# Four loads of softmax denominators stand at other places in a DMA queue

## The chip, the core and the metric

The kernel runs on one core of one Trainium2 chip. The metric is the device time of one execution in microseconds (us), as a median of several runs. The core has five engines with instruction queues of their own: PE (matrix multiply), DVE (vector), ACT (activation functions and copies), POOL (general) and SP, which in this kernel does nothing but issue DMA transfers. Each engine takes its instructions in the order in which they stand in its queue. An instruction that waits for a semaphore holds up all that stand behind it on the same engine.

## The reference

One transformer block over 2048 tokens of width 512, with sliding-window attention (32 heads of 16, window 256) and a gated feed-forward layer, both with shift, scale and gate vectors `sa, ca, ga, sb, cb, gb` computed from a condition vector:

```python
qkv = (x @ wqkv).reshape(B, S, 3, H, Dh).transpose(2, 0, 3, 1, 4)
q, k, v = qkv[0], qkv[1], qkv[2]
scores = jnp.einsum("bhqd,bhkd->bhqk", q, k) * (Dh ** -0.5)
mask = (idx[:, None] - idx[None, :] >= 0) & (idx[:, None] - idx[None, :] < W)
p = _softmax(jnp.where(mask[None, None], scores, -1e9), axis=-1)
o = jnp.einsum("bhqk,bhkd->bhqd", p, v)
...
h = _layernorm(x, axis=-1) * (1 + ca) + sa
x = x + ga * _A_ref(h, A_wqkv, A_wo)
h = _layernorm(x, axis=-1) * (1 + cb) + sb
x = x + gb * _B_ref(h, B_w1, B_w3, B_w2)
```

## The kernel before

The attention is cut into 32 units. Unit u belongs to head group g = u // 4 (four heads) and token block b = u % 4 (512 tokens). A unit has three parts, which run in different unit times:

- `unit_a(u)` makes queries and keys: 12 products on PE (L489), three copies on ACT (L495 the raw product, L501 and L498 the rounded parts `qk1` and `qk0`), two subtractions on POOL (L507), and then six transfers on SP (L512) that lay the parts out in `ring`, the buffer that the score products read.
- `unit_b(u)` finds the row maxima: 16 score products on PE (L542), a reduction for each on DVE (L549), two small DVE steps (L557, L559), a transpose (L565), a copy on ACT (L570) and two small transfers into `ring` (L574).
- `unit_c(u)` computes scores again (L819) with the maxima subtracted, masks them on POOL (L847, L864) or DVE, takes the exponential on ACT (L840), multiplies with the values on PE (L780), copies the result on ACT (L887) and stores it on SP (L890) to the DRAM tensor `o_dr[b]`.

Each head's stored result has 17 useful rows: 16 of the output, and row 16 (`DH`) with the sum of the exponentials, the denominator of the softmax.

The three parts are interleaved by a table of numbers. Each step has a key, 8 for each unit time plus an offset, and the steps with keys under `TS` = 232 are written out in the order of their keys; that order is what each engine's queue holds. While unit u runs its part c, unit u + 2 runs part b and unit u + 3 part a. Steps with later keys, and all of the output projection and the feed-forward layer behind them, are put in order by a scheduler at build time, `Sched`. Between the attention steps stand small side jobs: a load (L947 or L961), some work on POOL (L948 or L957) and a store (L949 or L962) of a piece of a later weight.

`early_sums` issues four loads (L791), one for each token block b: from `o_dr[b]` the denominators of the 28 heads of the first seven groups, 112 rows of 128 numbers, into a quarter of the tile `wqr`. The last of these 28 heads is stored by unit 24 + b, with the key 8(24 + b) + 10.63. The load before stands at the key 8(24 + b) + 12.5, so it is the next SP instruction behind that store. The next steps on SP are the side job's load and the six transfers L512 of the next `unit_a`, whose keys lie 4.8 to 5.2 behind the store's.

The four quarters of `wqr` are read in the stretch that `Sched` orders: a reciprocal on DVE (L1163) for each b, a store of the result (L1164) to `r_dr[b]`, and from there loads (L1176) that spread it over the rows of the output, which is then multiplied with it ahead of the output projection (L1205).

The store's key, and the keys of L512 and of the load:

```python
at(t0 + X["o"][1], store, "store", (["os"], [("o_dr", b, g)], 0.5, 256))
...
for r in range(3):
    at(t0 + y["row"][r], lambda r=r: rows(r), "qk_rows")
```

with `X["o"][1]` = 10.63 and t0 = 8u in `unit_c`, and `X["row"]` = (8.681, 8.806, 9.018) and t0 = 8(u − 3) − 1.228 in `unit_a`.

Of the kernel before, what the change touches and what calls it, by code (L numbers as in the profile page):

```python
# [21 lines left out]
NB = 4  # L22
# [26 lines left out]
NU = NQ * NB  # L49
# [231 lines left out]
def us(t):  # L281
# [5 lines left out]
             job_dma=("SP", 0.5), scores=("PE", 0.2), top=("DVE", 0.5), parts=("DVE", 0.4), turn=("PE", 0.11), cut=("ACT", 0.16),  # L287
# [36 lines left out]
def block_kernel(ctx: ExitStack, tc: tile.TileContext, x, wqk, wv, wo, w13, w2, c, wmod, out):  # L324
# [400 lines left out]
    def at(t, fn, kind=None, use=None):  # L725
        ops.append((t, len(ops), fn, kind))
# [57 lines left out]
    def early_sums(at):  # L784

        lt = {}
        for b in range(NB):
            def load(b=b):
                if not lt:
                    lt[0] = a1.tile([P, D], F32, name="wqr", bufs=1)  # L790
                nc.sync.dma_start(lt[0][:16 * NQ - 16, b * P:b * P + P], o_dr[b].rearrange(  # L791
                    "(h r) t -> h r t", r=32)[:H - 4, DH].rearrange("h (s t) -> h s t", t=P))
            at(8 * (NU - 2 * NB + b) + 12.5, load, "job_dma")
        return lt

    def unit_c(u, t0, at):
# [194 lines left out]
    for u in range(NU):  # L991
# [10 lines left out]
        if u in (2, 14):  # L1002
            at(8 * u + 0.3, lambda u=u: copy_raw(u // 14))
    firsts = early_sums(at)
    ops.sort(key=lambda o: o[:2])
    last = [o for o in ops if o[0] >= TS]
# [687 lines left out]
```

## Time and profile before

| | us |
|---|---|
| median of 3 runs | 974.34 (974.3 to 975.61) |
| the profiled execution, its own time | 971.44 |
| its span in the profile | 969.4 |
| mean granted clock of PE in it | 0.993 of full |

The profile lists one execution. Times in its rows are microseconds from the start of the span. "SPq" rows are DMA issues on SP: the start and the time that issuing took, not the transfer itself. In square brackets stands how long an engine was idle before a row, and what released it. The granted clock is the share of full speed that PE's throttle gave. Attention runs from about 40 to 482 us; the first store L890 is at 113 us, the 28th (unit 27) at 438.6 us.

### The profile page before, as it was taken

How to read it: one execution, taken by the hardware profiler on the slowest of the kernel's cores; microseconds unless marked ns; L12 is line 12 of the kernel's file. 1: busy time of each engine (PE TensorE's matmuls, PEld its weight loads, DVE VectorE, ACT ScalarE, POOL GpSimd, SP SyncE). 2: the span in 40 equal slices, each digit the busy share in tenths (PEclk: the TensorE clock that was granted, in tenths of full speed). 3: DMA queues.
4: the chain of work that ended last, by engine and by line, in shares of the span. 5: the costliest groups of instructions: out<-in, count | busy, mean ns of one | idle time of the engine just before them, and what ended most of it. 6: DMA issues, size and time to landing. Idle time of an engine off the chain costs nothing.

```text
span 969.4 us, 17140 instructions
## 1 busy us (share of the span) xinstructions
PE 939.2 (97%) x5316; PEld 717.3 (74%) x5316; DVE 720.6 (74%) x2041; ACT 552.2 (57%) x1258; POOL 524.4 (54%) x734
## 2 busy tenths in 40 slices
PE   6999999999999999998899999999999999999998
PEld 2678777777777776664588778888888888888886
DVE  6575889899989898977667695667679765566545
ACT  3333888787878787765669854433446343433330
POOL 7321787777868686754643774368556332222320
PEclk9999999999999999998999999999999999999999
DMA  9521354444544444435893664575554523212002
GB/s 312 175 78 56 111 184 145 144 143 144 170 150 143 144 144 144 135 126 166 227 261 115 202 206 158 185 253 200 171 168 173 171 90 93 65 63 83 34 23 87
DMA packets 81559, 141.64 MB, mean 146 GB/s; under 512 B 10554, under 2 KB 23226, under 8 KB 81468
## 3 DMA queue, kind: packets, MB, share of 16 engines
q1 hardware_dynamic: 80748, 139.50, 44.4%
q10 hardware_dynamic: 720, 1.05, 0.3%
q8 instruction: 42, 0.69, 0.3%
q14 instruction: 49, 0.40, 0.2%
HBM read 85.72 MB, written 34.61 MB: 124 GB/s over the span
## 4 chain that ended last, share of the span: by engine, by line
PE 83%; POOL 6%; DVE 4%; DMA 3%; issue 2%; ACT 1%; SPq 0%; POOLq 0%; ACTq 0%; DVEq 0%
PE st L1469 11%; PE mx L1469 11%; PE mx L542 7%; PE pj L489 7%; PE st L819 7%; PE mx L1563 6%; PE po L780 6%; PE st L1563 6%; PE po L1469 4%; PE st L709 3%; PE pj L1469 3%; POOL pt L847 2%; PE po L1563 2%; POOL qk L507 2%; PE mx L1205 2%
## 5 line engine op out<-in xcount | busy, mean ns | idle before, releaser
L549 DVE CUSTOM_DVE_ANT_0 junk<-mx,mskq 128x384 bf16<-128x384 f32 (+2 forms) x503 | 251.9, 527 | 31.2 <-PE mx L542 29.6
L542 PE MATMUL mx<-ring 96*128 96x384 f32 (+1 forms) x503 | 152.7, 342 | 6.2 <-DMA ring<-qk 3.5
L819 PE MATMUL st<-ring 100*128 100x384 f32 (+2 forms) x488 | 148.8, 346 | 0.5 <-ACT pt L840 0.4
L847 POOL TENSOR_SCALAR_AFFINE_SELECT pt<-pt 128x256 f32<-128x256 f32 x268 | 108.6, 408 | 69.2 <-ACT pt L840 58.7
L489 PE MATMUL pj<-hT,wq 128*128 128x512 f32 x384 | 136.7, 406 | 1.2 <-DVE wq L478 0.8
L542 PEld LDWEIGHTS mx<-ring 96*128 96x128 f32 x503 | 92.8, 191 | 38.4 <-DVE mt L549 23.2
L840 ACT ACTIVATE pt<-st 128x256 f32<-128x256 f32 x263 | 94.7, 387 | 36.5 <-DVE st L837 28.8
L1513 POOL TENSOR_TENSOR t<-t,t 128x512 f32<-128x512 f32 x28 | 41.0, 1463 | 137.6 <-DVE t L1501 133.8
L819 PEld LDWEIGHTS st<-ring 100*128 100x128 f32 x488 | 91.8, 192 | 18.5 <-issue 6.7
L780 PE MATMUL po<-pt,vS 128*17 128x256 f32 (+2 forms) x1408 | 98.2, 391 | 2.3 <-POOL pt L847 1.8
L507 POOL TENSOR_TENSOR qk<-qkr,qk 128x512 fp32r<-128x512 f32 x64 | 83.2, 1300 | 27.6 <-ACT qkr L495 27.3
L837 DVE COPY_PREDICATED st<-later,st 128x128 f32<-128x128 uint8 x263 | 71.0, 291 | 13.1 <-PE st L819 10.3
L489 PEld LDWEIGHTS pj<-hT,wq 128*128 128x128 f32 x384 | 71.8, 191 | 10.2 <-issue 1.7
L1060 POOL TENSOR_TENSOR w<-w,w 128x512 fp32r<-128x512 f32 (+2 forms) x35 | 55.5, 1599 | 34.0 <-PE pj L1563 17.8
L780 PEld LDWEIGHTS po<-pt,vS 128*17 128x17 f32 x1408 | 32.8, 97 | 47.7 <-issue 21.7
L1501 DVE TENSOR_TENSOR t<-mx,t 128x512 f32<-128x512 f32 x54 | 36.9, 687 | 37.3 <-PE mx L1469 34.3
L1469 PE MATMUL st<-b,w 128*128 128x512 f32 x240 | 60.2, 390 | 1.4 <-ACT t L1508 1.4
L864 POOL TENSOR_SCALAR_AFFINE_SELECT sm<-sm 128x256 f32<-128x256 f32 x109 | 41.9, 406 | 30.1 <-ACT sm L854 26.1
L1469 PE MATMUL mx<-b,w 128*128 128x512 f32 x228 | 57.1, 391 | 0.0
L831 ACT ACTIVATE pt<-st 128x384 f32<-128x384 f32 (+2 forms) x109 | 45.6, 434 | 14.2 <-DVE st L827 12.7
L1469 PEld LDWEIGHTS st<-b,w 128*128 128x128 f32 x240 | 45.0, 188 | 11.4 <-ACT t L1508 1.8
L1501 DVE TENSOR_TENSOR t<-st,t 128x512 f32<-128x512 f32 x35 | 24.1, 689 | 37.0 <-PE st L1469 33.3
(322 smaller groups left out, 2093.4 us busy)
## 6 DMA issues: line engine op xcount, KB each, us to landing
ring<-qk SPq DMA_DIRECT2D x192, 128.0 KB
o_dr<-os SPq DMA_DIRECT2D x32, 256.0 KB
w<-wsum SPq DMA_DIRECT2D x14, 512.0 KB
w<-w2g SPq DMA_DIRECT2D x14, 512.0 KB
jb<-in_w SPq DMA_DIRECT2D x24, 256.0 KB
wraw<-in_w SPq DMA_DIRECT2D x7, 768.0 KB
w<-wraw SPq DMA_DIRECT2D x14, 384.0 KB
vS<-in_wmod SPq DMA_DIRECT2D x20, 256.0 KB
```

Source lines behind the costliest of these rows:

```text
L489: nc.tensor.matmul(v["ps"], WQ[g][w][:, n // 3], hTp(i, n // 3, b * BT, BT), start=(n == 0), stop=(n == 3 * KC - 1))
L507: nc.gpsimd.tensor_tensor(out=v[n], in0=v["raw"], in1=v[1].bitcast(F32), op=ALU.subtract)
L542: nc.tensor.matmul(v[i][:, :n], queries(NS, a, gq, 1), keys(NS, hh, a, k0, gq + 1 - k0), start=True, stop=True)
L549: nc.vector.tensor_tensor_reduce(out=junk[:, :n], in0=v[i][:, :n], in1=mskq[:, 3 * P - n:], scale=1.0, scalar=-3e38, op0=ALU.add, op1=ALU. ...
L780: nc.tensor.matmul(po[32 * i:32 * i + DH + 1, qb * P:(qb + nq) * P], vS[:, kb, 4 * g + i], pts[i // 2][:, i % 2, c0:c0 + nq], start=first, ...
L819: nc.tensor.matmul(ps[:, :nq], keys(NM, hh, a, kb, 1), queries(NM, a, kb, nq), start=True, stop=not plus)
L837: nc.vector.copy_predicated(ps[:, 0], later, ps[:, 2])
L840: nc.scalar.activation(pt_of(j, a)[:, hh, :2], v[j, a, hh][:, :2], AF.Exp, scale=SCALE)
L847: nc.gpsimd.affine_select(out=pt[:, :, 2 * m], in_=pt[:, :, 0], **w)
L1469: nc.tensor.matmul(ps(bk), WT[s, n][w][:, col], BB[t, k][r], start=start and c == 0, stop=stop and c == 5, skip_group_check=True)
L1501: return nc.vector.tensor_add(o, x, y)
L1563: nc.tensor.matmul(ps(bk), tiles[hk + (h,)][:, i * P:(i + 1) * P], w2_of(last, y, f), start=(m == 0), stop=(m == 5))
```

## The change

The four loads get later keys. For b = 0, 1, 2 the key is 8 larger, one unit time; for b = 3 it is 3.4 larger, 231.9, which is just behind the last of the transfers L512 (231.79) and just under `TS`.

```diff
@@ early_sums
                 nc.sync.dma_start(lt[0][:16 * NQ - 16, b * P:b * P + P], o_dr[b].rearrange(
                     "(h r) t -> h r t", r=32)[:H - 4, DH].rearrange("h (s t) -> h s t", t=P))
-            at(8 * (NU - 2 * NB + b) + 12.5, load, "job_dma")
+            at(8 * (NU - 2 * NB + b) + (20.5 if b < NB - 1 else 15.9), load, "job_dma")
         return lt
```

SP's queue in units 24 and 25, before. `o_dr_74` to `o_dr_77` are `o_dr[0]` to `o_dr[3]`; `x2` is two equal issues in a row:

```order
L890 DMA o_dr_74<-os 128x512
L791 DMA wqr<-o_dr_74 112x1x128
L961 DMA jb_6935<-in_w 128x512
L512 DMA ring<-qk_6865 16x4x512 x2
L512 DMA ring<-qk_6831 16x4x512 x2
L512 DMA ring<-qk_6873 16x4x512 x2
L949 DMA w2g<-jb_6702 128x512
L574 DMA ring<-mT_7015 4x4x128 x2
L890 DMA o_dr_75<-os 128x512
L791 DMA wqr<-o_dr_75 112x1x128
L961 DMA jb_7170<-in_w 128x512
L512 DMA ring<-qk_7100 16x4x512 x2
```

And the same place now:

```order
L890 DMA o_dr_74<-os 128x512
L961 DMA jb_6933<-in_w 128x512
L512 DMA ring<-qk_6863 16x4x512 x2
L512 DMA ring<-qk_6831 16x4x512 x2
L512 DMA ring<-qk_6871 16x4x512 x2
L949 DMA w2g<-jb_6702 128x512
L574 DMA ring<-mT_7013 4x4x128 x2
L890 DMA o_dr_75<-os 128x512
L791 DMA wqr<-o_dr_74 112x1x128
L961 DMA jb_7169<-in_w 128x512
L512 DMA ring<-qk_7099 16x4x512 x2
```

Unit 24 has no load any more, and the load in unit 25 reads `o_dr[0]`, stored a unit earlier, instead of `o_dr[1]`, whose store stands right ahead of it. Units 26 and 27 follow in the same way, with `o_dr[1]` and `o_dr[2]`.

SP's queue in unit 27, up to the first loads for the output projection, before:

```order
L890 DMA o_dr_77<-os 128x512
L791 DMA wqr<-o_dr_77 112x1x128
L512 DMA ring<-qk_7545 16x4x512 x2
L512 DMA ring<-qk_7516 16x4x512 x2
L512 DMA ring<-qk_7553 16x4x512 x2
L1181 DMA wq_7629<-o_dr_74 128x1x512
L1137 DMA wo_7637<-wog 128x512
```

And now:

```order
L890 DMA o_dr_77<-os 128x512
L791 DMA wqr<-o_dr_76 112x1x128
L512 DMA ring<-qk_7544 16x4x512 x2
L512 DMA ring<-qk_7515 16x4x512 x2
L512 DMA ring<-qk_7552 16x4x512 x2
L791 DMA wqr<-o_dr_77 112x1x128
L1181 DMA wq_7629<-o_dr_74 128x1x512
L1137 DMA wo_7637<-wog 128x512
```

The third load now stands ahead of the six transfers, and the fourth between them and L1181. On the other engines the order of the instructions is the same as before.

## The prediction

> **What bounds the kernel now.** I read four views in turn: the page, PE's waits around the stretch that the change touches, SP's timeline there, and the granted clock in short windows. The page first:
>
> ```profile
> span 969.4 us, 17140 instructions
> PE 939.2 (97%) x5316; PEld 717.3 (74%) x5316; DVE 720.6 (74%) x2041; ACT 552.2 (57%) x1258; POOL 524.4 (54%) x734
> ```
>
> PE is busy for 97% of the span, so a change on SP's queue counts only where PE has run dry because of that queue. The longest of PE's waits between 380 and 540 us (in total, times, longest):
>
> ```profile
> PE st L542 <- DMA ring<-qk: 3.9, 1, 3.9
> PE mx L542 <- DMA ring<-qk: 2.4, 2, 1.7
> ```
>
> Three waits, 6.3 us together, are for the transfers of queries and keys into `ring`, which L512 issues on SP. They are these three rows of PE's timeline (idle before the row in brackets):
>
> ```profile
> 409.42 0.30 PE L542 MATMUL mx<-ring 96*128 96x128 f32 x1 [0.69 <-DMA ring<-qk]
> 422.77 0.41 PE L542 MATMUL mx<-ring 96*128 96x384 f32 x1 [1.71 <-DMA ring<-qk]
> 448.61 0.66 PE L542 MATMUL st<-ring 96*128 96x384 f32 x1 [3.85 <-DMA ring<-qk]
> ```
>
> Why are these transfers late? SP's timeline (start, duration): the first store L890, and then units 23 to 27, where unit n stands for the stretch that begins with the store of unit n:
>
> ```profile
> 113.38 0.43 SPq L890 DMA_DIRECT2D o_dr<-os  x1
> ...
> 387.37 0.43 SPq L890 DMA_DIRECT2D o_dr<-os  x1
> 387.90 0.37 SPq L947 DMA_DIRECT2D jb<-in_w  x1
> 389.67 3.89 SPq L512 DMA_DIRECT2D ring<-qk  x6
> ...
> 399.33 0.43 SPq L890 DMA_DIRECT2D o_dr<-os  x1
> 401.46 0.90 SPq L791 DMA_DIRECT2D wqr<-o_dr  x1
> 402.46 0.97 SPq L961 DMA_DIRECT2D jb<-in_w  x1
> 403.53 3.83 SPq L512 DMA_DIRECT2D ring<-qk  x6
> ...
> 411.91 0.44 SPq L890 DMA_DIRECT2D o_dr<-os  x1
> 414.04 0.86 SPq L791 DMA_DIRECT2D wqr<-o_dr  x1
> 415.00 0.48 SPq L961 DMA_DIRECT2D jb<-in_w  x1
> 415.58 3.82 SPq L512 DMA_DIRECT2D ring<-qk  x6
> ...
> 425.50 0.43 SPq L890 DMA_DIRECT2D o_dr<-os  x1
> 427.58 0.86 SPq L791 DMA_DIRECT2D wqr<-o_dr  x1
> 429.07 3.89 SPq L512 DMA_DIRECT2D ring<-qk  x6
> ...
> 438.63 0.44 SPq L890 DMA_DIRECT2D o_dr<-os  x1
> 441.57 0.87 SPq L791 DMA_DIRECT2D wqr<-o_dr  x1
> 442.55 3.81 SPq L512 DMA_DIRECT2D ring<-qk  x6
> ```
>
> In unit 23, without a load, L947 follows the store after 0.1 us. In the other four units SP stands still between the end of the store and L791 for 401.46 − 399.76 = 1.70, then 1.69, 1.65 and 2.50 us: the load reads what the store has just written and waits for it to land. Then it takes 0.87 us to issue. All that time L512 is queued behind it. What L512 itself needs first is ACT's copy into `qk0` (L498):
>
> ```profile
> 389.01 0.63 ACT L498 ACTIVATE qk<-pj 128x512 fp32r<-128x512 f32 x1
> 400.94 0.63 ACT L498 ACTIVATE qk<-pj 128x512 fp32r<-128x512 f32 x1
> 413.44 0.65 ACT L498 ACTIVATE qk<-pj 128x512 fp32r<-128x512 f32 x1
> 428.42 0.62 ACT L498 ACTIVATE qk<-pj 128x512 fp32r<-128x512 f32 x1
> 440.25 0.63 ACT L498 ACTIVATE qk<-pj 128x512 fp32r<-128x512 f32 x1
> ```
>
> In unit 23, L512 starts 0.03 us after L498's end (389.64), having left SP free for 1.40 us. In units 24, 25 and 27 it starts 1.96, 1.49 and 1.67 us after it; in unit 26 0.03 us after (that unit was itself late). So the loads delay the ring transfers in three units, the same three in which PE waits.
>
> **What the change does to this.** In unit 24 the load is gone from the queue. In units 25, 26 and 27 a load stays in its place but reads the store of the unit before, which has landed some 10 us earlier; of its cost the issue of 0.87 us and a gap of 0.1 us remain, the wait of 1.65 to 2.50 us goes. The fourth load stands behind unit 27's L512, where its store has been under way for over 5 us. The remaining 0.97 us fit into the 1.40 us that unit 23 shows free ahead of L512, so I cost them at nothing; if that cover were gone they would cost up to 0.97 us in each of three units. Behind L512 the fourth load holds up L1181 by the same 0.97 us, but it held that row up before too, so nothing is added.
>
> Does a later load starve its reader? The row of the view by tile:
>
> ```profile
> L1163 DVE RECIPROCAL wqr<-wqr x4: 889/942/948, 444.7 to 465.2; 112x128 f32<-112x128 f32 x4
> ```
>
> The first reciprocal is at 444.7 and will find the load of about 412; the last is at 465.2 and will find a load issued at about 445. Nothing here costs time.
>
> **The sum.** Where L512 starts on time, its third pair still needs the second POOL subtraction, L507:
>
> ```profile
> 402.98 1.30 POOL L507 TENSOR_TENSOR qk<-qkr,qk 128x512 fp32r<-128x512 f32 x1
> 415.49 1.29 POOL L507 TENSOR_TENSOR qk<-qkr,qk 128x512 fp32r<-128x512 f32 x1
> 442.29 1.28 POOL L507 TENSOR_TENSOR qk<-qkr,qk 128x512 fp32r<-128x512 f32 x1
> ```
>
> and the chain of waits shows when the last transfer started and how long it flew:
>
> ```profile
> 406.77 2.56 DMA ring<-qk
> 418.81 3.72 DMA ring<-qk
> 445.78 2.37 DMA ring<-qk
> ```
>
> Six issues take 3.83 us, so one takes 0.64, and the last can start 0.64 us after L507's end plus 0.03.
> Unit 24: 404.28 + 0.03 + 0.64 = 404.95 against 406.77, 1.82 us earlier; the wait of 0.69 goes whole.
> Unit 25: 416.78 + 0.67 = 417.45 against 418.81, 1.36 us earlier; of the wait of 1.71 us, 0.35 stay if the transfer again flies 3.72 us, nothing if it flies 2.56. I take 1.5 of 1.71 as gained.
> Unit 27: 443.57 + 0.67 = 444.24 against 445.78; 1.54 of the 3.85 us go. The other 2.3 belong to POOL, which is late next, and stay.
>
> The stalls also cost clock. Windows (length, busy of PE, PEld, DVE, ACT, POOL, granted clock, DMA share, GB/s):
>
> ```profile
> 420.60:424.00 3.40, 1.69 (x11) 1.27 (x8) 1.34 (x7) 1.24 (x3) 1.45 (x4) 0.92 0.22 81
> 424.00:427.30 3.30, 3.30 (x15) 2.86 (x17) 2.04 (x8) 2.06 (x7) 0.81 (x2) 0.57 0.22 84
> 448.60:452.00 3.40, 3.39 (x20) 1.62 (x20) 2.58 (x11) 0.00 (x0) 0.00 (x0) 0.50 0.83 233
> ```
>
> Right behind the stall of 1.71 us the clock falls to 0.57 for a full PE: 3.4 × 0.08 + 3.3 × 0.43 = 1.69 us of work lost, which does not happen when the stall is at most 0.35. Behind the stall of 3.85 us the clock stands at 0.50, and 3.4 × 0.50 = 1.7 us are lost in that window. A stall of 2.3 us is longer than the 1.71 that already cost clock, so most of this stays: between 0 and 1.7 us less are lost, and I take 0.5, nearer to the lower end.
>
> The Trainium skill, "TensorE: Matmul & The Clock Gate", section "What's actually happening", speaks against the first of these: it has the clock halved only after at least one idle window of about 3.4 us, and a stall of 1.71 us is half of that. By that rule the 1.69 us would not be the stall's doing and would not come back, and the sum below would be 3.6 to 3.8 us. The trace does not agree: the two windows show the lowered clock right behind this short stall.
>
> Up to unit 27's store the terms make 0.69 + 1.5 + 1.69 = 3.9 us. A check from the stores: 23 intervals from 113.38 to 387.37 are 11.91 us each, the three from 399.33 to 438.63 are 39.30 in all, 3.56 more than three of those. I take 3.5 of these, then 1.54 and 0.5: **5.5 us**. Behind 448.61 the order of all queues is as before, and SP's later transfers are released by the same rows that come earlier, so the gain should be carried to the end. The profiled execution took 971.44 us (span 969.4 and 2.0 around it) and would take 965.9; the runs shown have a median of 974.34, 2.9 above it, so I predict **968.8 us**.
>
> **Rivals.**
> *More is gained*: the 3.85 us also go nearly whole, because with the stretch before undisturbed POOL's L507 comes earlier against PE, and with it the later half-clock stretch. 6.25 + 1.69 + 1.7 = 9.6 us: 964.7. Against it: PE has no other work queued ahead of that wait, so the distance from ACT's copy over POOL to the ring is what it is.
>
> *The clock is not returned*: the window from 420.60 has PE busy for only 1.69 of 3.40 us, so the clock may fall for how the work lies in it rather than for the wait, and fall again. Then only the waits go, 0.69 + 1.36 + 1.54 = 3.6 us: 970.7. Against it: the fall to 0.57 stands behind the only wait of that stretch. The rule of the clock page named above would give this result too.
>
> *Nothing is kept*: either L512 proves bound by ACT and POOL, as in unit 26 where the load cost nothing, or PE, arriving earlier at the output projection, waits there for transfers. The DMA share of 0.83 beyond 448 us speaks for the second; that PE shows no wait for any such transfer up to 540 us speaks against it. 0 to 1.5 us: about 973.5.
>
> *Slower*: without the wait, the load goes out while the 256 KB store is still in flight, and 112 rows of 512 B mix with it just ahead of the ring transfers. If that is what made one transfer fly 3.72 instead of 2.37 us, 1.35 us are added in units 25, 26 and 27. It decides once the added flight exceeds the earlier start, 1.36 us, together with whatever is left of SP's 1.40 us of room. With both used up, PE loses 3 × 1.35 and two more half-clock stretches of 1.69, and gains back 0.69 and 1.54: 4.05 + 3.38 − 2.23 = 5.2 us, 979.5. Against it: before, too, the load went out just ahead of the ring transfers, and then it was nearer to them.
>
> That the load does not move is ruled out by the order of SP's queue.
>
> **How the numbers follow.** The forecast, with its own range of 967 to 971, has a chance of 0.55; more gained 0.08, the clock not returned 0.15, nothing kept 0.13, slower 0.09. The range is 965.0 to 973.8: it leaves out the slower case and little below. A measurement of this kernel tells a difference from none at about 0.2%, 1.95 us: faster than 972.4 are the first three, 0.78, and a small part of nothing kept, 0.02, together 0.80; within 0.2% the rest of it, 0.11; slower 0.09.
>
> **What would show it.** In the profile of the changed kernel, no standstill between L890 and L791 beyond 0.1 us; L512 starting within 0.1 us of L498's end in units 24 to 27; PE's waits for `ring<-qk` in units 24 and 25 gone or under 0.4 us, that in unit 27 at about 2.3 us; no granted clock below 0.9 between 409 and 440 us; store intervals near 11.9 us up to unit 27. The prediction is wrong if L512 starts on time and PE still waits, if a wait of the same size turns up behind 448 us, or if the ring transfers fly 3.7 us in every unit.

## The result, and the profile after

| | before, us | changed, us | ratio, 95% interval |
|---|---|---|---|
| median, 8 runs each | 974.13 (970.46 to 975.61) | 965.57 (963.11 to 969.48) | 0.9921 (0.9901 to 0.994) |
| the same again on another chip, 14 and 5 runs | 971.85 (970.15 to 975.87) | 967.59 (965.24 to 967.7) | 0.9948 (0.9929 to 0.9968) |
| the profiled execution's span | 969.4 | 963.9 | |

The ratios are worked out from all runs and are not quite the quotients of the medians. The change makes the kernel faster by 7.7 us by the first ratio (0.79% of 974.13) and by 5.1 us by the second; by the medians it is 8.6 and 4.3 us. The intervals overlap between 0.9929 and 0.994. The prediction was 968.8 us with a gain of 5.5 us, and the two profiled executions differ by 5.5 us. The first median, 965.57 us, lies below the forecast's own range of 967 to 971 and just inside the stated range, which begins at 965.0.

SP's timeline of the changed kernel, units 24 to 27 (start, duration of the issue):

```profile
398.96 0.43 SPq L890 DMA_DIRECT2D o_dr<-os  x1
399.49 0.37 SPq L961 DMA_DIRECT2D jb<-in_w  x1
401.22 4.34 SPq L512 DMA_DIRECT2D ring<-qk  x6
...
410.78 0.43 SPq L890 DMA_DIRECT2D o_dr<-os  x1
411.25 0.89 SPq L791 DMA_DIRECT2D wqr<-o_dr  x1
412.25 0.47 SPq L961 DMA_DIRECT2D jb<-in_w  x1
412.83 3.86 SPq L512 DMA_DIRECT2D ring<-qk  x6
...
422.22 0.43 SPq L890 DMA_DIRECT2D o_dr<-os  x1
422.70 0.87 SPq L791 DMA_DIRECT2D wqr<-o_dr  x1
424.52 3.89 SPq L512 DMA_DIRECT2D ring<-qk  x6
...
433.87 0.43 SPq L890 DMA_DIRECT2D o_dr<-os  x1
434.35 1.72 SPq L791 DMA_DIRECT2D wqr<-o_dr  x1
436.18 3.85 SPq L512 DMA_DIRECT2D ring<-qk  x6
```

ACT's copies into `qk0` in the same units:

```profile
400.56 0.63 ACT L498 ACTIVATE qk<-pj 128x512 fp32r<-128x512 f32 x1
412.15 0.65 ACT L498 ACTIVATE qk<-pj 128x512 fp32r<-128x512 f32 x1
423.86 0.63 ACT L498 ACTIVATE qk<-pj 128x512 fp32r<-128x512 f32 x1
435.50 0.64 ACT L498 ACTIVATE qk<-pj 128x512 fp32r<-128x512 f32 x1
```

Each load follows its store after 0.04 or 0.05 us, and each L512 starts 0.03 or 0.04 us after the copy's end (401.19, 412.80, 424.49, 436.14). The third load took 1.72 us to issue instead of 0.87, and still ended at 436.07, just inside the room.

All rows of PE's timeline between 410 and 450 us that show idle time before them:

```profile
436.88 0.45 PE L819 MATMUL st<-ring 100*128 100x384 f32 x1 [0.39 <-ACT pt L840]
442.07 0.41 PE L542 MATMUL st<-ring 96*128 96x384 f32 x1 [2.06 <-ACT pt L840]
```

The waits of 0.69 and 1.71 us are gone; the third, 3.85 us, is 2.06. Its row names ACT's L840, but that is not what PE waits for: when the same kernel was measured again the row had 2.14 us and named `ring<-qk`, and in a run below this product starts before that L840. The clock that had fallen behind the second wait does not fall any more. Windows of the changed kernel (columns as in the prediction):

```profile
420.60:424.00 3.40, 3.40 (x36) 2.23 (x35) 3.20 (x15) 3.26 (x11) 2.15 (x6) 1.00 0.22 82
424.00:427.30 3.30, 3.30 (x18) 2.88 (x19) 2.93 (x12) 2.46 (x8) 3.13 (x4) 1.00 0.36 115
```

Where is the gain along the span? The store of unit 28 in SP's timeline and the first row of the output projection in PE's timeline, first of the kernel before:

```profile
454.68 0.33 SPq L890 DMA_DIRECT2D o_dr<-os  x1
481.96 1.54 PE L1205 MATMUL mx<-wo,o 128*128 128x512 f32 x6
```

and of the changed kernel:

```profile
446.82 0.33 SPq L890 DMA_DIRECT2D o_dr<-os  x1
476.37 1.54 PE L1205 MATMUL mx<-wo,o 128*128 128x512 f32 x6
```

At unit 28's store the changed kernel is 7.86 us ahead (0.37 of them already at unit 23's, 387.37 against 387.00, ahead of anything that was changed), at the output projection 5.59, and from there to the end 5.5. So 2.3 us are given back between 447 and 476 us. The reason stands in the granted clock. The stretch from unit 28's store to the output projection, in the kernel before:

```profile
454.68:481.96 27.28, 23.82 (x193) 15.73 (x192) 20.47 (x58) 19.14 (x52) 17.36 (x27) 0.94 0.77 214
```

and in the changed kernel:

```profile
446.82:476.37 29.55, 26.08 (x194) 18.00 (x194) 20.56 (x58) 19.45 (x52) 17.37 (x27) 0.82 0.74 214
```

PE is idle for the same 3.46 and 3.47 us, and its two later waits (1.82 us for POOL, 1.65 us for DVE) are what they were. The same work takes 2.26 us longer at a clock of 0.82 instead of 0.94. In the short stretch ahead of it, from the end of the wait in unit 27 to unit 28's store, it is the other way round: 6.07 us at a clock of 0.54 before, 4.75 us at 0.67 now.

### The profile page after: what moved, and what is told of

The parts are those of the page before. It is cut to its first block, busy times and chain, and to the rows that moved or that the text cites. A ratio compares the mean times of both kernels' runs of the same rounds, so it can differ in the third digit from the quotient of the medians.

```text
span 963.9 us, 17134 instructions
## 1 busy us (share of the span) xinstructions
PE 938.2 (97%) x5316; PEld 717.5 (74%) x5316; DVE 720.3 (75%) x2041; ACT 552.2 (57%) x1258; POOL 524.9 (54%) x734
## 4 chain that ended last, share of the span: by engine, by line
PE 86%; DVE 4%; POOL 4%; DMA 2%; issue 2%; ACT 1%; SPq 0%; POOLq 0%; DVEq 0%; ACTq 0%
PE st L1469 11%; PE mx L1469 11%; PE pj L489 7%; PE mx L542 7%; PE st L819 7%; PE po L780 7%; PE mx L1563 6%; PE st L1563 6%; PE po L1469 4%; PE st L709 4%; PE pj L1469 3%; PE po L1563 2%; PE mx L1205 2%; PE pj L1563 2%; POOL pt L847 2%
## 5 line engine op out<-in xcount | busy, mean ns | idle before, releaser
L840 ACT ACTIVATE pt<-st 128x256 f32<-128x256 f32 x263 | 94.3, 386 | 36.2 <-DVE st L837 28.1
L507 POOL TENSOR_TENSOR qk<-qkr,qk 128x512 fp32r<-128x512 f32 x64 | 83.3, 1301 | 27.6 <-ACT qkr L495 27.4
L837 DVE COPY_PREDICATED st<-later,st 128x128 f32<-128x128 uint8 x263 | 71.0, 291 | 13.4 <-PE st L819 10.6
```

What stands on the lines that cost most here:

```text
L507: nc.gpsimd.tensor_tensor(out=v[n], in0=v["raw"], in1=v[1].bitcast(F32), op=ALU.subtract)
L837: nc.vector.copy_predicated(ps[:, 0], later, ps[:, 2])
L840: nc.scalar.activation(pt_of(j, a)[:, hh, :2], v[j, a, hh][:, :2], AF.Exp, scale=SCALE)
```

## The experiments

The theory is that of the prediction: a load costs what it makes L512 start late behind L498's end, as PE idle time and then as lost clock. Each time is a median, each ratio is to the kernel before in runs on the same chip, and gains in microseconds are by the ratio where nothing else is said.

**Which of the moved loads brings the gain?** First the fourth load left at its old place:

```diff
-            at(8 * (NU - 2 * NB + b) + (20.5 if b < NB - 1 else 15.9), load, "job_dma")
+            at(8 * (NU - 2 * NB + b) + (20.5 if b < NB - 1 else 12.5), load, "job_dma")
```

> The loads for b = 0, 1, 2 one unit later as in the change, the fourth at its old place. Theory (a load costs what it makes L512 start late behind L498's end): units 24 to 26 as in the changed kernel, no PE wait for the ring there; in unit 27 the fourth load waits about 2.5 us for its store and L512 starts about 1.6 us late, so PE's wait there grows from 2.1 to about 3.7 us. Time 1.5 to 3.3 us above the changed kernel (the upper end with one more half-clock window): 967 to 969. Rival (the gain comes from the fourth load, by what it lets go in the last attention units): near the kernel before, 972 to 974.

968.76 us, ratio 0.9958 (0.9942 to 0.9973), 4.1 us faster than before and inside the expected range. SP's and PE's timelines of this run in unit 27:

```profile
435.62 3.77 SPq L791 DMA_DIRECT2D wqr<-o_dr  x2
439.49 1.95 SPq L512 DMA_DIRECT2D ring<-qk  x3
...
445.65 0.66 PE L542 MATMUL st<-ring 96*128 96x384 f32 x1 [4.38 <-DMA ring<-qk]
```

Two loads, one of them waiting, hold SP for 3.9 us, and PE's only wait for the ring between 380 and 450 us is this one, 4.38 us. That is more than the 3.85 us of the kernel before, because this edit puts the third load into unit 27 as well: L512 starts 2.09 us after L498's end, where it had been 1.67.

Then the opposite, only the fourth load moved:

```diff
-            at(8 * (NU - 2 * NB + b) + (20.5 if b < NB - 1 else 15.9), load, "job_dma")
+            at(8 * (NU - 2 * NB + b) + (12.5 if b < NB - 1 else 15.9), load, "job_dma")
```

> Only the fourth load behind unit 27's L512, the other three at their old places. Theory: PE waits for the ring of about 0.7 and 1.7 us in units 24 and 25 and the half-clock window behind them stay, the wait of 3.9 us in unit 27 falls to about 2.2; time 1.5 to 3.5 us under the kernel before, 970.5 to 972.5. Rival (the fourth load carries the gain): 966 to 968.

969.16 us, ratio 0.9962 (0.9948 to 0.9976): 3.7 us faster, within neither theory's range in microseconds by the median and a little more than mine allowed. Its waits are as the theory has them, in PE's timeline:

```profile
409.43 0.30 PE L542 MATMUL mx<-ring 96*128 96x128 f32 x1 [0.84 <-DMA ring<-qk]
422.89 0.42 PE L542 MATMUL mx<-ring 96*128 96x384 f32 x1 [1.85 <-DMA ring<-qk]
446.99 0.41 PE L542 MATMUL st<-ring 96*128 96x384 f32 x1 [2.14 <-DMA ring<-qk]
```

The fourth load is worth 1.71 us of wait in this profile. The clock behind it returns 0.95 us more: from the end of this wait to the output projection it is 32.40 us here and 33.35 before. Together that is 2.7 us; the profiled execution as a whole is 2.5 us shorter than that of the kernel before. The rest of the 3.7 lies between executions, since the kernel before took 971.44 us in its profile and 972.96 in the median of this chip. Within their intervals the two halves, 4.1 and 3.7 us, add up to either measurement of the whole change, 7.7 and 5.1 us; they can't say more than that each has a share.

**Is it the place or the traffic?** All four loads in their own unit, but behind its ring transfers:

```diff
-            at(8 * (NU - 2 * NB + b) + (20.5 if b < NB - 1 else 15.9), load, "job_dma")
+            at(8 * (NU - 2 * NB + b) + 15.9, load, "job_dma")
```

> All four loads in their own unit, behind its six ring transfers instead of one unit later; by then the store has landed, so SP should not stand still for them. Theory: L512 starts within 0.1 us of L498's end in all four units; same time as the changed kernel within 2 us, 964 to 967.5. Rival (what counts is the traffic that the load's small packets make beside the ring transfers): the load now goes out while the last ring transfers fly, flights above 3 us and PE waits of 0.5 to 1.5 us come back, 968 to 971.

967.63 us, ratio 0.9947 (0.9932 to 0.9963): 0.13 us above the expected range in time, and the same ratio as the second measurement of the change, 0.9948. L512 starts 0.02 to 0.03 us after L498's end in all four units and PE does not wait for the ring in units 24 to 26. The loads now go out while the last ring transfers fly, and no wait comes back: traffic beside the ring transfers costs PE nothing here. How long the transfers fly is not measured where PE does not wait for them.

**Do the issues that stay cost anything?** All four loads behind unit 27:

```diff
-            at(8 * (NU - 2 * NB + b) + (20.5 if b < NB - 1 else 15.9), load, "job_dma")
+            at(8 * (NU - 2 * NB + NB - 1) + 15.9 + 0.01 * b, load, "job_dma")
```

> All four loads behind unit 27's L512, none in units 24 to 26. Theory: L512 on time in units 24 to 27, so up to unit 27 as the changed kernel; but three more issues of 0.9 us stand ahead of the first loads of the output projection, and the first reciprocal on DVE, which stands in its queue at about 439 us, now waits until the first load lands at about 443 us, holding DVE for up to 3 us: 965.5 to 969. Rival (the issues left in units 25 to 27 still cost PE time in the changed kernel): faster than it by 1 to 3 us, 962.5 to 964.5.

967.13 us, ratio 0.994 (0.9923 to 0.9957). It is no faster than the change. As this edit could also lose time in another place, the stores are the better witness: the three intervals from unit 24's to unit 27's sum to 34.85 us here and to 34.91 in the changed kernel. So the issues that the change leaves in units 25 and 26 cost no time that can be measured; unit 27 follows below. The reader is now starved, as DVE's timeline shows:

```profile
444.49 0.95 DVE L1163 RECIPROCAL wqr<-wqr 112x128 f32<-112x128 f32 x1 [2.65 <-DMA wqr<-o_dr]
```

DVE stands for 2.65 us, and even that shows in no time. A likely reason is that PE is itself in its wait for unit 27's ring until 443.76 in this run, so that little new work for DVE comes in; that was not tested. PE's and ACT's timelines of this run also settle what PE waits for in unit 27:

```profile
443.76 0.66 PE L542 MATMUL st<-ring 96*128 96x384 f32 x1 [1.99 <-DMA ring<-qk]
445.67 0.66 ACT L840 ACTIVATE pt<-st 128x256 f32<-128x256 f32 x2 [3.94 <-DVE st L837]
```

L840 stands behind the reciprocal by way of DVE's L837, and PE's product starts 1.9 us before it. So the product does not need L840, which the changed kernel's row named. The wait ends 8.13 us after unit 27's store here and 8.20 in the changed kernel: the load that the change leaves there costs next to nothing, and what stays of the wait is the way over the ring.

**Is it the standstill for the store, or any delay of L512?** The changed kernel with extra loads of `o_dr` in units 24 to 26, ahead of the ring transfers, that wait for nothing (`more` loads 96 rows into quarters of the tile that are overwritten later):

```diff
-            at(8 * (NU - 2 * NB + b) + (20.5 if b < NB - 1 else 15.9), load, "job_dma")
+            at(8 * (NU - 2 * NB + b) + (20.5 if b < NB - 1 else 15.9), load, "job_dma"); [at(8 * (NU - 2 * NB + b) + 12.5, lambda b=b, c=c: more(b, c), "job_dma") for c in range(256, 512, 128) if b < NB - 1]
```

> The changed kernel with two more loads of 96 rows in units 24, 25 and 26 ahead of the ring transfers, which wait for nothing and whose data are overwritten later. Theory: SP's room of 1.4 us is overdrawn by 0.5 us in unit 24 and by 1.5 us in units 25 and 26; L512 starts late by that much. PE has about 1 us of slack behind L512, so waits of 0 to 0.7 us come back in units 25 and 26; 0.3 to 2 us above the changed kernel, 966 to 967.5. Rival (only the standstill for the store costs, issues are hidden whatever their number): no PE wait, same time within 0.3 us.

969.28 us, ratio 0.9955 (0.9939 to 0.9972), above the expected range. SP's timeline in unit 25 with ACT's copy, and the one wait of PE for the ring in units 24 to 26:

```profile
411.97 0.86 SPq L791 DMA_DIRECT2D wqr<-o_dr  x1
412.88 1.61 SPq L786 DMA_DIRECT2D wqr<-o_dr  x2
414.59 0.46 SPq L961 DMA_DIRECT2D jb<-in_w  x1
415.15 1.29 SPq L512 DMA_DIRECT2D ring<-qk  x2
...
413.02 0.64 ACT L498 ACTIVATE qk<-pj 128x512 fp32r<-128x512 f32 x1
...
422.25 0.58 PE L542 MATMUL mx<-ring 96*128 96x384 f32 x1 [1.64 <-DMA ring<-qk]
```

L512 is 415.15 − 413.66 = 1.49 us late, to the hundredth what it was in this unit before, and PE waits 1.64 us where it had waited 1.71, though nothing in the queue waits for a store. In this unit a delay ahead of L512 costs the same, whichever cause it has. In unit 24 of this run L512 is 0.65 us late (402.36 against 401.71) and no wait follows, so PE has some slack there. My expectation was wrong in the slack: I gave PE 1 us, and unit 25 has none. The extra loads add traffic as well as delay, but the change itself leaves one load just ahead of L512 in this unit, on time, and PE does not wait. The last transfer flies 3.69 us there in the chain of waits, as it flew 3.72 before.

The same with four extra loads in each of these units (`range(256, 512, 64)`, half the size):

> As the run with two more loads, but four more in each of units 24, 25 and 26, of half the size. Theory: L512 late by about 2.5 us in unit 24 and 3.4 us in units 25 and 26, PE waits of about 1.3, 2.3 and 2.3 us and a half-clock window of 1.7 us behind two or three of them: 8 to 11 us above the changed kernel, 974 to 977, no better than the kernel before although no load waits for a store. Rival (only the standstill for the store costs): below 968.

972.5 us, ratio 0.9994 (0.9979 to 1.0008): the whole gain is undone without any wait for a store, with L512 in unit 27 as much on time as in the change (0.03 us after the copy). L512 is 2.87 us late in unit 24 and 3.07 in unit 25. PE's timeline:

```profile
410.32 0.30 PE L542 MATMUL mx<-ring 96*128 96x128 f32 x1 [1.71 <-DMA ring<-qk]
425.36 0.66 PE L542 MATMUL mx<-ring 96*128 96x384 f32 x1 [3.40 <-DMA ring<-qk]
```

The time is 1.5 us under the expected range: unit 26, late itself by then, adds no third wait, and the first wait cost no clock (see the last section).

**Is there more of the kind in the queue?** In the changed kernel six loads L943 stand between the second and the third pair of ring transfers, in the stretches that end with the stores of units 2, 6, 10, 14, 18 and 22. Moved behind the third pair:

```diff
-            at(8 * u + 7.65, lambda u=u: gate_load(int(u > 6)))
+            at(8 * u + 7.9, lambda u=u: gate_load(int(u > 6)))
```

> The changed kernel with the six gate loads L943, which stand between the second and third pair of ring transfers in units 2 to 22, moved behind the third pair. Theory: the third pair starts up to 0.6 us earlier in these units, the PE wait of 0.8 us for the ring in unit 22 goes: 0.3 to 1.5 us faster than the changed kernel, about 964.8. Rival (the third pair waits for POOL's second subtraction anyway, the ring is not late there): same within 0.3 us.

962.12 us, ratio 0.9881 (0.9865 to 0.9897), faster than I expected. PE's wait in the last of these stretches in the changed kernel,

```profile
372.70 0.42 PE L542 MATMUL mx<-ring 96*128 96x384 f32 x1 [0.76 <-DMA ring<-qk]
```

and in this one:

```profile
371.46 0.42 PE L542 MATMUL mx<-ring 96*128 96x384 f32 x1 [0.35 <-DMA ring<-qk]
```

That is the largest of the six; waits of 0.28 to 0.53 us at the same place ahead of the stores of units 6, 10, 14 and 18, put down to DVE or to "issue" in the profile, are gone too. Since this is the best version, it was measured again beside the changed kernel, and the same edit was tried on the kernel before.

> The changed kernel once more, on the chip of the two runs beside it. Theory: 965 to 967, and where its profile differs from the first one in time by a microsecond or two, the granted clock between 440 and 470 us differs with it.

> The changed kernel with the six gate loads behind the third pair of ring transfers, once more, beside the changed kernel on one chip. Theory (the third pair was held by the gate load in six units): again 2.5 to 4 us below the changed kernel, 961.5 to 963.5. Rival (the first measurement owed part of its gain to another chip): 1.5 us or less below it.

> The kernel before, without the change, with the six gate loads behind the third pair. Theory (both edits free the same queue in different units, so their gains add): 2.5 to 4 us below the kernel before, about 970. Rival (the gate loads matter only once units 24 to 27 run freely): within 1 us of the kernel before.

| on one chip | us | ratio to before, 95% interval |
|---|---|---|
| the change | 967.59 | 0.9948 (0.9929 to 0.9968) |
| the change and the gate loads moved | 962.66 | 0.99 (0.9877 to 0.9923) |
| the gate loads moved alone | 969.22 | 0.9968 (0.9953 to 0.9984) |

Both edits together are 4.9 us below the change alone by the medians, a little more than expected; the gate loads alone gain 3.1 us. With 5.1 us for the change that makes 8.2, and 9.7 us were measured for both: within the intervals they add. The store intervals bear it out: the six that end with these stores sum to 74.43 us with the change (second measurement) and to 70.13 us with both. All 23 intervals up to unit 23's store sum to between 273.7 and 275.0 us in the nine profiles without this edit, and to between 271.3 and 272.1 in the three with it. The change's own second measurement is 0.6 us above its expected range; its profiled span is 965.6 us, 1.7 more than the first one's. Of these, 0.7 are there at the wait in unit 27 (it ends at 442.78 instead of 442.07); the rest arises up to the output projection, and the granted clock from 440 to 470 us is 0.72 where the first one had 0.77.

## Why the prediction was right

*L512 is held by the load's standstill.* Right, and shown: L512 starts with L498's end in all four units, and extra loads that delay it by the same 1.49 us bring nearly the same wait back, 1.64 us for 1.71.

*The remaining issues cost nothing; no reader is starved.* Right: without them units 24 to 26 take the same time, and even a reader starved by 2.65 us shows no loss.

*Units 24 to 26, taken as 3.5 us.* Too small by 0.9. The three intervals between the stores of units 24 and 27 fell from 39.30 to 34.91 us, 4.4 us. The terms had made 3.9; I cut them to 3.5 by the check against the mean of 11.91 us over 23 units. That mean was itself raised by the gate loads of six of those units: without these six it is 11.80, and the check would have made 3.9 too. The other half of the gap is that the undisturbed intervals here are shorter still, 11.82, 11.44 and 11.65 us; the wait of 1.71 us went whole, where I had taken 1.5. The clock term was right for this profile: the window at 0.57 is at 1.00, and the rival by which the clock would not come back falls. But that a wait of this size costs clock is itself a matter of where it lies (see the last section); another execution of the kernel before need not lose these 1.69 us.

*The wait in unit 27, 1.54 of 3.85 us.* Right in kind, 1.79 measured. What stays is bound by the ring, as predicted. That POOL is what holds it is not shown apart from SP's own pace: L507 ends at 438.82 us, and at 0.64 us an issue the third pair could not go out before 438.74.

*The clock behind unit 27, 0.5 us gained, and the gain carried unchanged to the end.* This is the term that was mis-sized. The part between the wait and unit 28's store did gain, 1.32 us (6.07 against 4.75), but the stretch behind it lost 2.27 (27.28 against 29.55): 0.95 us lost instead of 0.5 gained. In the sum of the profile, 0.37 us of difference ahead of unit 24 that the change did not make, 4.4 for units 24 to 26, 1.8 for the wait and −0.95 for the clock make 5.6 us at the output projection. So 0.9, 0.25 and 0.37 too little in front and 1.45 too much behind nearly cancelled: the mechanism was right, but that the profiled gain is 5.5 us to the tenth is luck. In the runs as a whole the gain was 5.1 and 7.7 us, on both sides of the 5.5.

*The other rivals.* The wait in unit 27 did not go whole, so "more is gained" had the wrong mechanism, though the first measured median lies 0.9 us from its 964.7. No new wait of PE for a transfer appeared up to 540 us, against "nothing is kept". That the load's traffic makes the kernel slower falls with the change itself, where the load goes out just ahead of L512 and PE does not wait in units 24 to 26. In unit 25 the flight is 3.7 us with the wait for the store and, in the run with two extra loads, without it. What makes it longest in that unit was not tried.

## What to carry to other kernels

A DMA that reads what the instruction just ahead of it writes holds up its whole queue until the write has landed, here for 1.65 to 2.50 us. Put it behind what the busy engine needs next, or a turn later, and look at the start of the queued transfer against the end of its real producer: that difference is the delay, whether it comes from a wait or from mere issues. What the busy engine feels of it depends on its slack: 1.96 us late cost PE 0.69 us in unit 24, and 1.49 us late cost 1.71 in unit 25. Then look along the same queue for other transfers of no urgency in the same place; here those were worth another 3 to 5 us. A mean over earlier turns is no floor as long as some of them have the same fault. And a gain of 5 to 8 us in 970 needs many runs: two profiles of the same kernel differ here by 1.7 and 1.8 us.

## What the runs showed of the hardware

In these runs a short wait of PE cost clock or not by where it lay. When the profiles are read from 395 to 482 us in pieces of 0.1 us, the granted clock is 1.00 or 0.50 everywhere but in the pieces in which it changes. In the kernel before it falls at 423.45, 447.34 and 464.41 us and returns at 426.86, 454.17 and 467.82. The distances, 3.41, 20.48, 6.83, 10.24 and 3.41 us, are all whole multiples of 3.41 us, and so they are within each of the twelve profiles. In these traces the clock thus changes only at the edges of windows of 3.41 us, and a profile shows where these edges lie. They lie at other places in each execution.

The wait of 1.71 us before lay from 421.06 to 422.77, whole within such a window, which had PE busy for 1.70 us, and the next one ran at half clock:

```profile
420.04:423.45 3.41, 1.70 (x22) 0.95 (x14) 1.32 (x6) 1.01 (x3) 2.01 (x5) 1.00 0.35 121
423.45:426.87 3.42, 3.42 (x12) 3.13 (x11) 2.17 (x9) 2.09 (x6) 0.81 (x2) 0.50 0.15 56
```

With the gate loads moved alone even a wait of 2.22 us cost no clock:

```profile
420.88 0.41 PE L542 MATMUL mx<-ring 96*128 96x384 f32 x1 [2.22 <-DMA ring<-qk]
```

An edge of that run lies at 419.62, in the middle of the wait. The two windows that share it had 2.47 and 2.15 us of work, and the clock stayed:

```profile
416.20:419.62 3.42, 2.47 (x28) 0.89 (x27) 2.53 (x13) 2.16 (x5) 2.99 (x8) 1.00 0.60 204
419.62:423.03 3.41, 2.15 (x12) 1.97 (x13) 1.65 (x6) 1.09 (x4) 0.68 (x2) 1.00 0.02 6
423.03:426.44 3.41, 3.41 (x36) 2.32 (x35) 2.85 (x14) 2.80 (x7) 2.45 (x5) 1.00 0.22 84
```

The wait of 1.71 us in the run with four extra loads, ending at 410.32, ran 0.12 us past an edge at 410.20; its window had 1.82 us of work, and the clock stayed. Over all twelve profiles in this stretch, the clock fell after every window at full clock with 1.79 us or less of PE work, after none with 2.47 or more, and after two of the four between. It returned only after a window with at least 3.25 us of work, but five windows filled whole were not followed by its return; why not stays open.

The Trainium skill, "TensorE: Matmul & The Clock Gate", section "What's actually happening", says that the clock is set by the activity in windows of about 3.4 us that run freely and do not start anew with the kernel. The 3.41 us and the edges of these traces agree. Its other statement, that the clock is halved after at least one idle window, does not: a window that was half idle was enough.

A gain in front of a stretch with short waits therefore moves these waits against the windows, and one or two microseconds come or go there by chance. The same kernel shows it: the change with the gate loads moved, from unit 28's store to the output projection, in its two profiles:

```profile
446.13:473.62 27.49, 24.03 (x194) 16.55 (x191) 20.18 (x58) 19.35 (x52) 17.40 (x27) 0.88 0.79 224
445.94:475.44 29.50, 26.04 (x194) 17.96 (x194) 20.56 (x58) 19.46 (x52) 17.36 (x27) 0.82 0.71 199
```

PE is idle for 3.46 us in both; the whole difference of 2.01 us is busy time of PE, at a clock of 0.82 instead of 0.88.
